# Infini-attention plus SiLU layer on one core: tile 2 of x issued from ScalarE, VectorE's constants made behind the norms

## The chip, the core and the metric

The kernel runs on one core of one Trainium2 chip. A core has five engines with instruction queues of their own, each of which runs in program order: TensorE (PE; its weight loads are shown as PEld), VectorE (DVE), ScalarE (ACT), GpSimd (POOL) and SyncE (SP), which here only issues transfers. ScalarE can issue transfers as well. Engines wait for each other and for transfers through semaphores. The metric is the device time of one execution in microseconds (us); the time of a kernel is the median over several runs.

## The reference, cut to what matters

A sequence of 2048 tokens of width 512 is normalised; an attention with 32 heads of width 16, in four segments of 512 tokens with a memory that is carried from segment to segment, and a dense layer with SiLU both read the normalised x, and both are added to x.

```python
x = A_x
xn = _layernorm(x, axis=-1)
return x + _A_ref(xn, A_wq, A_wk, A_wv, A_wo, A_beta) + _B_ref(xn, B_w1, B_w2)
...
for s in range(N):
    qs, ks, vs = (q[:, :, s].copy(), k[:, :, s].copy(), v[:, :, s].copy())
    p = _softmax(jnp.einsum('bhqd,bhkd->bhqk', qs, ks) * scale + mask, axis=-1)
    a_dot = jnp.einsum('bhqk,bhkd->bhqd', p, vs)
    pq = phi(qs)
    num = jnp.einsum('bhld,bhde->bhle', pq, M)
    den = jnp.einsum('bhld,bhd->bhl', pq, z)[..., None] + 1e-06
    outs.append(g * num / den + (1.0 - g) * a_dot)
    pk = phi(ks)
    M = M + jnp.einsum('bhld,bhle->bhde', pk, vs)
    z = z + jnp.einsum('bhld->bhd', pk)
...
out = jnp.einsum('bsf,fd->bsd', _silu(jnp.einsum('bsd,df->bsf', x, w1)), w2)
```

x, the weights and the result are bf16; wq, wk, wv and wo are 512 x 512, w1 is 512 x 1792 and w2 1792 x 512.

## The kernel before

x is cut into 16 tiles of 128 tokens, four to a segment. Each tile is normalised on VectorE, turned so that its 512 channels lie on partitions (`xnT`), and multiplied with wq, wk, wv and w1 in pieces of 128 channels. The scores of a segment are made in batches, go through an exponential on ScalarE (line 730), are masked on GpSimd (line 744) and weigh v (line 791). Everything is accumulated in on-chip banks and copied out by VectorE or ScalarE.

The order of work is a list written out by hand, `ORDER`. Each word is a piece of work: a short function that issues one instruction or a few, on one or more engines. Each engine then executes its own instructions in the order of the list. The words that matter here are these:

- `xc`, `xd`: the statistics of a tile and their aggregate, on VectorE (lines 286 and 289); `xs` does both at once; `xq`, `xi`: square root on ScalarE (line 303) and reciprocal on VectorE (line 306); `Nv`: the normalised tile, on VectorE (line 315). `xg4.4` makes the roots of tiles 4 to 7 together on GpSimd (lines 297 and 300), and `xs4` to `xs7` are their statistics.
- `X`, `Xa`, `Xv`: the transposes of a tile on TensorE (line 845), and their copies into `xnT` on ScalarE or VectorE (line 851).
- `busy`: matmuls on zeros that fill TensorE's time (line 864). `busy44` stands ahead of the first transposes, `X0.1`.
- `v`, `k`, `q`, `h`: products of line 336; `vv`, `va`, `kv`, `ka`, `qv`, `qa`: their copies on VectorE or ScalarE (lines 376, 399 and 406). `kf0.0` splits the first k (lines 392 and 393) and needs `pm_odd` and `pm_even`; `kp` does the same on GpSimd for later ones.
- `S`: a batch of scores; `E`, `O`: weighted sums.
- `kind`: five small VectorE instructions on 128 x 1 numbers (lines 239 to 246), first used for the sums of the denominators; `odd`: the two reductions that make `pm_odd` and `pm_even` (lines 223 and 224); `omask`: one conversion of `pm_odd` (line 235), first used when the odd sums are merged (line 835).
- `ones0`, `ones1`, `zeros`: memsets on GpSimd.

Ahead of the list stand the loads. Tiles 0 to 3 are loaded one by one by `load_x`, 128 KB each, in turn from SyncE's queue and ScalarE's. On SyncE's queue follow wv in two halves, wk, wq, tiles 4 to 7 (`x_hi`), w1 in two halves, tiles 8 to 11 and 12 to 15, and beta, each issued as soon as a semaphore of an earlier transfer is free. ScalarE loads its table and runs one activation ahead of its first use (line 190) after its own issues; VectorE clears `zraw` (line 188) and `lows` (line 262) ahead of the list.

Of the kernel before, what the change touches and what calls it, by code (L numbers as in the profile page):

```python
# [13 lines left out]


ORDER = """
kind odd omask ones0 ones1 zeros xc0 xd0 xc1 xq0 xi0 Nv0 busy44 xd1 xq1 xc2 xi1 X0.1 Nv1 xd2 Xa0.1 busy6 v0.0.0 v0.0.1 xq2 X1.1 Xa1.1 xs3 xi2 Nv2 v0.0.2 xq3 v0.0.3 xi3 v0.1.0 v0.1.1 Nv3 X2.1 va0.0 k0.0.0 k0.0.1 tb Xv2.1 X3.1 v0.1.2 v0.1.3 Xv3.1 vv0.1 k0.1.0 k0.0.2 k0.0.3 ka0.0 fp0.0 kf0.0 q0.0.0 q0.0.1 q0.0.2 q0.0.3 xs4 k0.1.1 qa0.0 k0.1.2 k0.1.3 kv0.1 fa0.0 xs7
S0 k0.3.0 fa0.1 k0.2.0 k0.2.1 k0.2.2 k0.2.3 kv0.2 k0.3.1 k0.3.2 q0.1.0 xs5 xs6 xg4.4 fv0.0 k0.3.3 kv0.3
S2 q0.1.1 v0.2.0 kp0.1 q0.1.2 q0.1.3 qv0.1 v0.2.1 v0.2.2 v0.2.3 vv0.2 fa0.2 Nv6 Nv4 XD6 XD4 h0.0.0 h0.0.1
S1 Nv5 XD5 h0.0.2 h0.0.3 ha0.0 hv0.0 h0.1.0 h0.1.1 fp0.2 h0.1.2 h0.1.3 q0.2.0  # L20
S3 q0.2.1 q0.2.2 q0.3.0 q0.3.1 q0.3.2 q0.2.3 Nv7 qv0.2 ha0.1 h0.2.0 h0.2.1 kp0.2 q0.3.3
# [72 lines left out]
def kernel(  # L94
# [13 lines left out]
    nc = tc.nc  # L108
# [10 lines left out]
    TPS = L // P  # L119
# [24 lines left out]
    def xs(t0, t1):  # L144
        if t0 >= NT - TPS:
            return x_end[:, t0 - NT + TPS : t1 - NT + TPS, :]
        return x_lo[:, t0:t1, :] if t1 <= TPS else x_hi[:, t0 - TPS : t1 - TPS, :]
# [9 lines left out]
    def load_x(eng, t0, n):  # L157
        eng.dma_start(
            out=xs(t0, t0 + n),
            in_=x_flat[t0 * P : (t0 + n) * P, :].rearrange("(n p) d -> p n d", p=P),  # L160
        )

    load_x(nc.sync, 0, 1)
    load_x(nc.scalar, 1, 1)
    load_x(nc.sync, 2, 1)
    load_x(nc.scalar, 3, 1)

    def load_w(eng, w_sb, W, k0, k1):
        eng.dma_start(out=w_sb[:, k0:k1, :], in_=W.rearrange("(ko ki) n -> ki ko n", ki=P)[:, k0:k1, :])
# [45 lines left out]
    kind = cpool.tile([P, 1], F32, name="kind")  # L215
# [16 lines left out]
    omask = cpool.tile([P, 1], I32, name="omask")  # L232
# [710 lines left out]
```

## Time and profile before

| | |
|---|---|
| median of 3 runs | 221.12 us (220.74 to 221.27) |
| the profiled execution | 220.8 us, of which the span from its first to its last instruction is 219.1 us |
| TensorE busy | 211.6 us, 4019 matmuls |
| ScalarE busy | 184.2 us |
| VectorE busy | 181.0 us |
| GpSimd busy | 126.8 us |
| granted TensorE clock | 1.00 |
| transfers | 19.60 MB, mean 89 GB/s |

The page gives busy time by engine, then the chain of waits: from the last instruction back, at each step to what released it. A row of the timeline has the start and the length in us, the engine, the line, the operation, the tile written and the tiles read, their sizes and the count; in brackets stands the idle time of the engine ahead of it and what ended that. Rows of an engine overlap a little where its instructions are pipelined. Windows give the busy time of each engine in a stretch of the span.

### The profile page before, as it was taken

How to read it: one execution, taken by the hardware profiler on the slowest of the kernel's cores; microseconds unless marked ns; L12 is line 12 of the kernel's file. 1: busy time of each engine (PE TensorE's matmuls, PEld its weight loads, DVE VectorE, ACT ScalarE, POOL GpSimd, SP SyncE). 2: the span in 40 equal slices, each digit the busy share in tenths (PEclk: the TensorE clock that was granted, in tenths of full speed). 3: DMA queues.
4: the chain of work that ended last, by engine and by line, in shares of the span. 5: the costliest groups of instructions: out<-in, count | busy, mean ns of one | idle time of the engine just before them, and what ended most of it. 6: DMA issues, size and time to landing. Idle time of an engine off the chain costs nothing.

```text
span 219.1 us, 9343 instructions
## 1 busy us (share of the span) xinstructions
PE 211.6 (97%) x4019; PEld 116.3 (53%) x4042; DVE 181.0 (83%) x370; ACT 184.2 (84%) x173; POOL 126.8 (58%) x203
## 2 busy tenths in 40 slices
PE   7999999999999999999999999999999999999994
PEld 7666655556544544445544445455454544465663
DVE  7899999999897878757988979777899798669364
ACT  3899989999999999999999999999999988860000
POOL 6039986679687845695845486667768473410000
PEclk9999999999999999999999999999999999999999
DMA  6994549242003035321122142160032221322313
GB/s 197 357 372 128 79 129 344 42 79 46 4 4 75 25 86 71 83 62 29 51 74 61 43 121 28 47 79 7 4 99 75 75 76 45 97 60 76 97 52 97
DMA packets 33273, 19.60 MB, mean 89 GB/s; under 512 B 14672, under 2 KB 33232, under 8 KB 33232
## 3 DMA queue, kind: packets, MB, share of 16 engines
q1 hardware_dynamic: 30608, 16.39, 29.1%
q10 hardware_dynamic: 2624, 2.62, 3.7%
q8 instruction: 31, 0.51, 1.0%
q14 instruction: 10, 0.08, 0.1%
HBM read 9.96 MB, written 2.10 MB: 55 GB/s over the span
## 4 chain that ended last, share of the span: by engine, by line
PE 82%; DVE 9%; POOL 4%; issue 2%; ACT 1%
PE ps L336 20%; PE psO L338 16%; PE ps L338 15%; PE psS L724 9%; PE psO L336 9%; PE psV L791 8%; PE psS L338 4%; DVE stats L286 2%; POOL Pb L744 2%; DVE Vz L406 1%; POOL k L385 1%; DVE hT L497 1%; DVE pk L433 1%; POOL lows L744 1%; PE ptr L845 1%
## 5 line engine op out<-in xcount | busy, mean ns | idle before, releaser
L730 ACT ACTIVATE Pb<-psS 128x2048 bf16<-128x2048 f32 x72 | 135.2, 1877 | 6.3 <-PE psS L724 4.1
L744 POOL TENSOR_SCALAR_AFFINE_SELECT Pb<-Pb 128x512 bf16<-128x512 bf16 (+2 forms) x88 | 61.6, 710 | 19.2 <-ACT Pb L730 16.5
L497 DVE SCALAR_TENSOR_TENSOR hT<-th,ps 128x512 bf16<-128x512 bf16 x56 | 38.0, 681 | 10.6 <-ACT th L492 10.2
L744 POOL TENSOR_SCALAR_AFFINE_SELECT lows<-Pb 64x512 bf16<-64x512 bf16 (+1 forms) x40 | 23.2, 581 | 37.5 <-ACT Pb L730 31.1
L338 PE MATMUL psO<-w_sb,hT 128*32 128x512 bf16 (+2 forms) x708 | 43.3, 321 | 0.0
L336 PE MATMUL ps<-xnT,w_sb 128*128 128x512 bf16 (+1 forms) x165 | 34.2, 329 | 0.4 <-DVE Vz L406 0.2
L492 ACT ACTIVATE th<-ps 128x512 bf16<-128x512 f32 x56 | 33.2, 594 | 1.7 <-PE ps L338 1.6
L338 PEld LDWEIGHTS <-hT 128*32 128x32 bf16 x876 | 21.6, 97 | 14.0 <-issue 2.6
L338 PE MATMUL ps<-xnT,w_sb 128*32 128x512 bf16 (+1 forms) x448 | 26.4, 348 | 0.0
L724 PE MATMUL psS<-qT,k 32*128 32x64 bf16 (+3 forms) x512 | 23.0, 233 | 0.5 <-ACT Pb L730 0.3
L336 PEld LDWEIGHTS <-w_sb 128*128 128x128 bf16 x168 | 15.8, 98 | 11.4 <-issue 1.0
L791 PE MATMUL psV<-Pb,Vz 128*32 128x448 bf16 (+7 forms) x512 | 21.6, 286 | 0.2 <-POOL Pb L744 0.2
L724 PEld LDWEIGHTS <-k 32*128 32x128 bf16 x512 | 9.4, 92 | 22.8 <-issue 22.2
L336 PE MATMUL psO<-w_sb,hT 128*128 128x512 bf16 (+2 forms) x82 | 20.9, 326 | 0.6 <-issue 0.5
L791 PEld LDWEIGHTS <-Vz 128*32 128x32 bf16 x768 | 16.2, 97 | 9.2 <-issue 0.8
L621 DVE SCALAR_TENSOR_TENSOR o_out<-psO,x_res 128x512 bf16<-128x512 f32 x14 | 9.6, 689 | 6.6 <-PE psO L338 4.9
L338 PEld LDWEIGHTS <-w_sb 128*32 128x32 bf16 x448 | 11.2, 96 | 7.3 <-issue 1.6
L724 PE MATMUL psS<-qT,kT 16*128 16x448 bf16 (+3 forms) x256 | 14.7, 269 | 0.0
L821 DVE CAST oraw<-psV 128x512 bf16<-128x512 f32 x15 | 10.2, 682 | 3.1 <-PE psV L791 3.0
L406 DVE CAST Vz<-ps 128x512 bf16<-128x512 f32 x15 | 10.2, 682 | 2.8 <-PE ps L338 1.6
L336 PEld LDWEIGHTS <-hT 128*128 128x128 bf16 x89 | 7.8, 98 | 8.7 <-issue 2.2
L336 PE MATMUL ps<-xnT,wq_sb 128*128 128x256 bf16 (+1 forms) x59 | 12.1, 322 | 0.2 <-issue 0.2
(113 smaller groups left out, 333.5 us busy)
## 6 DMA issues: line engine op xcount, KB each, us to landing
spr<-rz SPq DMA_DIRECT2D x56, 64.0 KB
x_res<-in_A_x_dram SPq DMA_DIRECT2D x16, 128.0 KB
out_dram<-o_out SPq DMA_DIRECT2D x15, 128.0 KB
w_sb<-in_B_w_dram SPq DMA_DIRECT2D x2, 896.0 KB
w_sb<-in_B_w_dram ACTq DMA_DIRECT2D x1, 1792.0 KB
x_hi<-in_A_x_dram SPq DMA_DIRECT2D x2, 512.0 KB
wv_sb<-in_A_wv_dram SPq DMA_DIRECT2D x2, 256.0 KB
wk_sb<-in_A_wk_dram SPq DMA_DIRECT2D x1, 512.0 KB
```

The source lines that it names most:

```text
L286: nc.vector.bn_stats(out=stats[t][:], in_=xs(t, t + 1)[:, 0, :])
L336: return [nc.tensor.matmul(out, lhsT=lhsT, rhs=rhs, start=start, stop=stop, skip_group_check=True)]
L338: nc.tensor.matmul(out[c : c + 32], lhsT=lhsT[:, c : c + 32], rhs=rhs, start=start, stop=stop, tile_position=(0, c), skip_group_check=True,)
L406: copy(out=Vzs[s % 2][:, j, :, 0:3:2, :], in_=sts[s].pop(("v", j))[:, :].rearrange("p (h r d) -> p h r d", r=2, d=DH),)
L492: nc.scalar.activation(out=th[:], in_=sts[s]["h", ft][:, :], func=AF.Tanh, scale=0.5)
L497: nc.vector.scalar_tensor_tensor(out=st["hT"][:, ft, :], in0=st.pop(("th", ft))[:], scalar=1.0, in1=st.pop(("h", ft))[:, :], op0=ALU.add, ...
L621: out = nc.vector.scalar_tensor_tensor(out=o_out[:], in0=st.pop(("psO", j)), scalar=0.5, in1=st["x", j][:], op0=ALU.mult, op1=ALU.add)
L724: nc.tensor.matmul(psS[:, g, c : c + q2 - q1], lhsT=keys[rows], rhs=st["qT"][rows, dt, q1:q2], start=True, stop=True, tile_position=(32 * ...
L730: exp = nc.scalar.activation(out=blocks(Pb, b).rearrange("p y g c -> p g y c"), in_=psS[:, :, :].rearrange("p g (y c) -> p g y c", c=BLOCK ...
L744: over[id(Pb)].append(nc.gpsimd.affine_select(out=out, in_=in_, compare_op=ALU.is_ge, fill=0.0, base=base, pattern=[[0, out.shape[1]], [1, ...
L791: nc.tensor.matmul(psV[32 * g : 32 * g + 32, q0 : q0 + nq].rearrange("p (y c) -> p y c", y=weights.shape[2]), lhsT=Vzs[s % 2][:, kt, 4 * d ...
L821: copy(out=oraw[:], in_=sts[s].pop(("psV", 0))[:, :])
```

## The change

Two edits. First, tile 2 of x is no longer issued by SyncE behind tile 0 but by ScalarE behind tile 1; ScalarE issues tiles 1, 2 and 3, and wv is second on SyncE's queue. Second, the words `kind`, `odd` and `omask` leave the head of the list. `odd` goes behind `Xv3.1`, the copy of tile 3's transposes; `omask` and `kind`, in this order, go behind `S0`, the first batch of scores. On VectorE that puts `odd` between the copy of tile 3 and the copy `vv0.1`, and `omask` and `kind` between the statistics of tile 7 (`xs7`) and the copy `kv0.2`. All other words keep their order, and TensorE's, GpSimd's and ScalarE's own instructions keep theirs but for the extra issue. Long lines of the list are cut.

```diff
 ORDER = """
-kind odd omask ones0 ones1 zeros xc0 xd0 xc1 xq0 xi0 Nv0 busy44 xd1
+ones0 ones1 zeros xc0 xd0 xc1 xq0 xi0 Nv0 busy44 xd1
...
-v0.1.2 v0.1.3 Xv3.1 vv0.1 k0.1.0 k0.0.2 k0.0.3 ka0.0 fp0.0 kf0.0
+v0.1.2 v0.1.3 Xv3.1 odd vv0.1 k0.1.0 k0.0.2 k0.0.3 ka0.0 fp0.0 kf0.0
...
 q0.0.0 q0.0.1 q0.0.2 q0.0.3 xs4 k0.1.1 qa0.0 k0.1.2 k0.1.3 kv0.1 fa0.0 xs7
-S0 k0.3.0 fa0.1 k0.2.0 k0.2.1 k0.2.2 k0.2.3 kv0.2 k0.3.1 k0.3.2 q0.1.0 xs5 xs6 xg4.4 fv0.0 k0.3.3 kv0.3
+S0 omask kind k0.3.0 fa0.1 k0.2.0 k0.2.1 k0.2.2 k0.2.3 kv0.2 k0.3.1 k0.3.2 q0.1.0 xs5 xs6 xg4.4 fv0.0 k0.3.3 kv0.3
...
     load_x(nc.sync, 0, 1)
-    load_x(nc.scalar, 1, 1)
-    load_x(nc.sync, 2, 1)
-    load_x(nc.scalar, 3, 1)
+    for t in range(1, TPS):
+        load_x(nc.scalar, t, 1)
```

More of the change, by code (lines that the diff above doesn't have):

```diff
@@ L16 @@
 ORDER = """
-kind odd omask ones0 ones1 zeros xc0 xd0 xc1 xq0 xi0 Nv0 busy44 xd1 xq1 xc2 xi1 X0.1 Nv1 xd2 Xa0.1 busy6 v0.0.0 v0.0.1 xq2 X1.1 Xa1.1 xs3 xi2 Nv2 v0.0.2 xq3 v0.0.3 xi3 v0.1.0 v0.1.1 Nv3 X2.1 va0.0 k0.0.0 k0.0.1 tb Xv2.1 X3.1 v0.1.2 v0.1.3 Xv3.1 vv0.1 k0.1.0 k0.0.2 k0.0.3 ka0.0 fp0.0 kf0.0 q0.0.0 q0.0.1 q0.0.2 q0.0.3 xs4 k0.1.1 qa0.0 k0.1.2 k0.1.3 kv0.1 fa0.0 xs7
-S0 k0.3.0 fa0.1 k0.2.0 k0.2.1 k0.2.2 k0.2.3 kv0.2 k0.3.1 k0.3.2 q0.1.0 xs5 xs6 xg4.4 fv0.0 k0.3.3 kv0.3
+ones0 ones1 zeros xc0 xd0 xc1 xq0 xi0 Nv0 busy44 xd1 xq1 xc2 xi1 X0.1 Nv1 xd2 Xa0.1 busy6 v0.0.0 v0.0.1 xq2 X1.1 Xa1.1 xs3 xi2 Nv2 v0.0.2 xq3 v0.0.3 xi3 v0.1.0 v0.1.1 Nv3 X2.1 va0.0 k0.0.0 k0.0.1 tb Xv2.1 X3.1 v0.1.2 v0.1.3 Xv3.1 odd vv0.1 k0.1.0 k0.0.2 k0.0.3 ka0.0 fp0.0 kf0.0 q0.0.0 q0.0.1 q0.0.2 q0.0.3 xs4 k0.1.1 qa0.0 k0.1.2 k0.1.3 kv0.1 fa0.0 xs7
+S0 omask kind k0.3.0 fa0.1 k0.2.0 k0.2.1 k0.2.2 k0.2.3 kv0.2 k0.3.1 k0.3.2 q0.1.0 xs5 xs6 xg4.4 fv0.0 k0.3.3 kv0.3
 S2 q0.1.1 v0.2.0 kp0.1 q0.1.2 q0.1.3 qv0.1 v0.2.1 v0.2.2 v0.2.3 vv0.2 fa0.2 Nv6 Nv4 XD6 XD4 h0.0.0 h0.0.1
```

## The prediction, made before the changed kernel ran

> **What bounds the kernel now.** I read the page's first part, then its chain of waits, then the same chain from 10 to 46 us, then the timeline of the first 17 us, where every moved instruction lies.
>
> ```profile
> span 219.1 us, 9343 instructions
> PE 211.6 (97%) x4019; PEld 116.3 (53%) x4042; DVE 181.0 (83%) x370; ACT 184.2 (84%) x173; POOL 126.8 (58%) x203
> PE 82%; DVE 9%; POOL 4%; issue 2%; ACT 1%
> ```
>
> TensorE is busy for 97% of the span and carries 82% of the chain that ended last. The windows of busy time (engines in the order PE, PEld, DVE, ACT, POOL, then clock, DMA share, GB/s) show where the other 18% can come from:
>
> ```profile
> 38.00:120.00 82.00, 80.86 (x1535) 41.72 (x1548) 68.87 (x138) 80.47 (x70) 57.68 (x89) 1.00 0.24 54
> 120.00:200.00 80.00, 79.42 (x1594) 40.59 (x1596) 67.16 (x131) 71.46 (x65) 45.46 (x71) 1.00 0.25 61
> ```
>
> From 38 to 200 us TensorE idles 1.1 us of 82 and 0.6 of 80. Its order is fixed, so a time won or lost before 38 us has no idle stretch to vanish in: I carry it to the end one to one. The question is what sets the start of that packed part. The chain in order of time (start, length, what):
>
> ```profile
> 13.68 0.02 issue
> 13.71 0.69 DVE kT L376
> ...
> 16.10 0.58 POOL rstd_all L297
> ...
> 25.59 1.10 POOL Pb L744
> ...
> 27.07 0.69 DVE oraw L821
> ...
> 37.10 0.61 DVE Vz L406
> 37.71 0.14 issue
> 37.85 1.91 PE ps L336 x15
> ```
>
> So before 13.68 the chain is TensorE and ScalarE, from 13.71 to 16.0 it is VectorE, from 16.10 to 26.7 GpSimd, from 27 to 37.7 VectorE, and then TensorE. The stretch 13.71 to 16.0 is the one the change touches: the copy kv0.2, the statistics xs5 and xs6, and behind them GpSimd's root xg4.4.
>
> **The change part by part.** The head first (timeline, start and length in us):
>
> ```profile
> 1.10 4.17 PE L864 MATMUL psS<-zraw 128*128 128x128 bf16 x44 [1.10 <-DVE zraw L188]
> 1.40 1.23 DVE L262 MEMSET lows<- 64x1408 uint32 x1 [0.35 <-issue]
> 2.66 0.22 DVE L239 TENSOR_REDUCE kind<-ident 128x1 f32<-128x64 bf16 x1
> 2.91 0.15 DVE L243 TENSOR_SCALAR evec<-kind 128x1 f32<-128x1 f32 x1
> 2.98 0.14 DVE L244 TENSOR_SCALAR evec<-kind 128x1 f32<-128x1 f32 x1
> 3.16 0.16 DVE L245 TENSOR_TENSOR evec<-evec,evec 128x1 f32<-128x1 f32 x1
> 3.24 0.15 DVE L246 TENSOR_SCALAR sign<-kind 128x1 f32<-128x1 f32 x1
> 3.30 0.15 DVE L223 TENSOR_REDUCE pm_odd<-b 128x1 f32<-128x4 f32 x1
> 3.48 0.15 DVE L235 CAST omask<-pm_odd 128x1 int32<-128x1 f32 x1
> 3.56 0.68 DVE L286 BATCH_NORM_STATS2 stats<-x_lo 128x6 f32<-128x512 bf16 x1
> 5.55 0.66 DVE L286 BATCH_NORM_STATS2 stats<-x_lo 128x6 f32<-128x512 bf16 x1
> 5.60 0.40 PE L845 MATMUL ptr<-ident,xn_t 128*128 128x128 bf16 x4 [0.32 <-DVE xn_t L315]
> 6.73 0.66 DVE L286 BATCH_NORM_STATS2 stats<-x_lo 128x6 f32<-128x512 bf16 x1
> ```
>
> Eight small instructions stand between the memset, which ends at 2.63, and tile 0's statistics at 3.56: VectorE could start 0.9 us sooner. Two things cap that. TensorE first runs its 44 filler matmuls, which end at 5.27; the transposes of tile 0 start at 5.60, so TensorE can gain 0.33 us at most. And tile 0 must have landed. The windows from the start give bytes:
>
> ```profile
> 0.00:2.70 2.70, 1.59 (x16) 1.60 (x17) 1.44 (x3) 0.99 (x1) 1.90 (x12) 1.00 0.30 103
> 0.00:3.70 3.70, 2.60 (x25) 2.60 (x26) 2.37 (x11) 1.49 (x2) 2.90 (x13) 1.00 0.51 153
> 0.00:4.70 4.70, 3.60 (x37) 3.60 (x38) 3.33 (x13) 1.63 (x3) 3.48 (x15) 1.00 0.60 181
> 0.00:9.90 9.90, 8.26 (x81) 6.50 (x83) 8.09 (x29) 5.57 (x12) 3.48 (x15) 1.00 0.83 267
> ```
>
> By 2.70 us 2.7 x 103 = 278 kB are in, tiles 0 and 1 (262 kB); so tile 0 lands between 2.7 and 3.56. The full 0.33 us needs its statistics by 3.56 - 0.33 = 3.23, inside that interval and nearer its middle than its end: I take 0.33, with nothing as the other end.
>
> Tile 2 leaves SyncE's queue for a third place on ScalarE's. These rows say what an issue costs and who stands behind it:
>
> ```profile
> 0.78 0.90 ACTq L158 DMA_DIRECT2D x_lo<-in_A_x_dram  x2
> 0.79 0.87 SPq L158 DMA_DIRECT2D x_lo<-in_A_x_dram  x2
> 1.71 1.28 ACT L190 ACT_TABLE_LOAD   x1 [1.71 <-PEq L927]
> 4.55 0.29 ACT L303 ACTIVATE rstd_all<-mv_all,eps 128x1 f32<-128x1 f32 x1 [1.35 <-DVE mv_all L289]
> ```
>
> An issue is about 0.45 us. ScalarE's table load and its first activation move from 1.71 to 2.16 and end near 3.65; the first root, at 4.55 - 0.33 = 4.22, does not feel it. Without that cover of 0.57 us the 0.45 would go into tile 0's path. On SyncE everything behind tile 0 (wv, wk, wq, x_hi, w1 and the rest) is issued 0.44 us earlier. If both queues get equal shares, tile 2 is in after tiles 0 and 1, itself and as much of wv: 524 kB, 3.6 us by the second row; tile 3 after 786 kB, 4.4 us by the third (851 kB at 4.70). Their statistics, now at 5.55 and 6.73, would start at 5.22 and 6.40. Both are covered, tile 2 by 1.6 us less its landing delay. That delay is bounded by tile 0's: 0 to 0.86.
>
> Of the constants the two sums of pm_odd and pm_even (3.30 to 3.48, so 0.18 us) go behind the copy Xv3.1. They cost nothing, because VectorE waits 0.61 us just after; the other six go to the bad place (VectorE, 11 to 16 us):
>
> ```profile
> 11.04 0.35 DVE L392 TENSOR_SCALAR k<-kT,pm_odd 128x512 bf16<-128x512 bf16 x1 [0.61 <-ACT kT L376]
> 11.30 0.69 DVE L286 BATCH_NORM_STATS2 stats<-x_hi 128x6 f32<-128x512 bf16 x1
> 13.42 0.18 DVE L289 BATCH_NORM_AGGREGATE mv_all<-stats 128x2 f32<-128x6 f32 x1
> 15.03 0.18 DVE L289 BATCH_NORM_AGGREGATE mv_all<-stats 128x2 f32<-128x6 f32 x1
> 15.13 0.66 DVE L286 BATCH_NORM_STATS2 stats<-x_hi 128x6 f32<-128x512 bf16 x1
> 16.10 0.57 POOL L297 TENSOR_SCALAR rstd_all<-mv_all 128x4 f32<-128x4 f32 x1 [0.45 <-DVE mv_all L289]
> ```
>
> Omask and the five of kind now stand between the aggregate at 13.42 and kv0.2 at 13.71. They take, start to start, 3.30 - 2.66 = 0.64 for kind and 3.56 - 3.48 = 0.08 for omask: 0.72 us. Unpipelined, their lengths add up to 0.97; I take 0.72, since the same six issue back to back again. The idle time there: an aggregate's successor can start 0.10 us after it (15.03 to 15.13), so kv0.2 could have started at 13.52 and waited 0.19 for TensorE. The rest of the cover is the head's gain as far as VectorE still has it. It loses some at 11.30, since xs4 needs x_hi. Tiles, wv, wk, wq and x_hi are 5 x 524 kB = 2.62 MB, in by 9.9 us (267 x 9.9 = 2.64), so x_hi lands between 9.9 and 11.30; s, what xs4 can move forward, lies between 0.33 and 0. I take 0.2, near the middle, for want of a row that shows the landing.
>
> The sum at kv0.2: 0.72 - 0.19 - 0.2 = +0.33 us; its ends are 0.72 - 0.19 - 0.33 = +0.20 and 0.97 - 0.19 - 0 = +0.78. A gain is excluded as long as those six instructions must run there: 0.72 exceeds 0.19 + 0.33. Behind kv0.2 VectorE has no gap up to xs6, and GpSimd has already idled 0.45 us for xg4.4; so its chain to 26.7, VectorE's to 37.7 and TensorE's start at 37.85 each come 0.33 later. That makes the span 219.4, the profiled execution 221.1 (now 220.8 around a span of 219.1), and, against the median of the three runs, which is 0.3 above the profiled one, 221.4.
>
> One rule speaks against expecting more of the freed SyncE queue. The Trainium skill (DMA: Bandwidth & Descriptors, Issuing engines are not separate DMA queues) says that transfers started by different engines interleave on the same DMA engines, and that a second issuing engine saves issue time alone. The trace agrees: from 3.70 to 9.90 us the DMA share was (9.9 x 0.83 - 3.7 x 0.51) / 6.2 = 1.02, full. By the rule x_hi lands no earlier than today; if the 0.44 us of issue did bring it forward, s would be 0.33 and the sum +0.20.
>
> **The rivals.** Slower: tile 3 arrives late behind two others on ScalarE's queue. If SyncE's queue, always full, took three quarters of the engines at 300 GB/s, tiles 2 and 3 would pass at 75 GB/s from 2.7 us: 2 x 131 kB take 3.5 us, to 6.2, and with 0.86 for landing tile 3 is there at 7.06, 0.33 behind today's 6.73. The head is then 0.33 later instead of earlier, and kv0.2 is 0.72 - 0.19 + 0.33 = +0.86: 222.0. It decides once tile 3's statistics start after 6.73. For it: nothing in the trace shows how two full queues share; against: two tiles to a queue, all four were in by 3.70 (566 kB against 524).
>
> Faster: the VectorE stretch isn't what releases the packed part, GpSimd and VectorE catch up, and TensorE keeps its head gain: 0.33 less, 220.8. For it: VectorE is only 9% of the chain, and up to 13.68 TensorE sets it. Against: the 0.45 us that GpSimd waited for exactly these statistics, and no pause in GpSimd's chain of 10 us.
>
> The change doesn't do what it says: tile 0 lands only at about 3.56, the head gains nothing, and the constants cost 0.72 - 0.19 = +0.53: 221.65. For it: nothing shows the landing; against: 278 kB by 2.70.
>
> **How the numbers follow.** Forecast 0.58, no head gain 0.10, late tile 0.15, head gain kept 0.12; 0.05 for what I don't see, on either side. A measurement of this kernel can tell about 0.3%, 0.66 us, from no change. Of the forecast a tenth lies above that (its upper end is +0.78), and the late tile does: with half of the unseen, slower 0.24. A gain of 0.66 is twice the head's cap: half of the unseen and a quarter of the kept head, where one measurement also falls low, make faster 0.06. The same is left with 0.70. The forecast with its ends is 221.3 to 221.9 by the median; 220.6 to 222.1 takes in the kept head gain and the late tile.
>
> **What would show it.** Right: tile 0's statistics near 3.2 and the first transposes near 5.27; six small instructions between xs7's aggregate and kv0.2; kv0.2 near 14.04, GpSimd's root near 16.43, TensorE's long group near 38.2, and the same distance at the end. Wrong: statistics of tile 3 after 6.73 (late tile); kv0.2 at 13.8 or before, or the root late with the group at 37.85 on time (head gain kept); first transposes still at 5.60 (no head gain). A shift that grows after 38 us would break the one-to-one step.

## The result, and the profile after

The changed kernel takes 222.10 us (median of 12 runs, 221.61 to 223.21) against 221.18 us of the kernel before in the same session: a ratio of 1.0047 with an interval of 1.0034 to 1.0060. By the ratio it is 1.04 us slower (0.0047 x 221.2), by the two medians 0.92; +0.33 was forecast.

The first part of the changed kernel's page (all its line numbers are one lower than before's, since the calls of `load_x` lost a line; kernels with the old loads have before's numbers, and those that load halves have numbers seven higher):

```profile
span 220.8 us, 9345 instructions
PE 212.2 (96%) x4019; PEld 117.0 (53%) x4042; DVE 180.8 (82%) x370; ACT 184.2 (83%) x173; POOL 126.9 (57%) x203
```

The profiled execution took 222.54 us. The span is 1.7 us longer; TensorE is busy 0.6 us longer and the other three as long as before within 0.2. What grew is mostly waiting. Its chain of waits from 5 to 46 us, in order of time (start, length, what):

```profile
1.72 6.09 DMA x_lo<-in_A_x_dram
7.84 0.71 DVE stats L285
...
9.30 0.40 PE ptr L844 x4
...
11.51 0.60 ACT kT L375
...
15.36 0.60 DVE kT L375
...
17.66 0.57 POOL rstd_all L296
...
28.83 0.69 DVE oraw L820
...
39.60 1.91 PE ps L335 x15
```

The same stations as before, each later: the first copy of kT on ScalarE 11.51 for 10.42, the root 17.66 for 16.10, the first weighted sum `oraw` 28.83 for 27.07, the long group 39.60 for 37.85. Between the copy on ScalarE and `oraw` lies kv0.2, which starts at 15.28 in the timeline; the chain shows only its part from 15.36. The changed kernel's timeline (start, length, engine, line, operation, tiles, count, in brackets what ended the idle time before):

```profile
3.29 0.69 DVE L285 BATCH_NORM_STATS2 stats<-x_lo 128x6 f32<-128x512 bf16 x1 [0.66 <-DMA x_lo<-in_A_x_dram]
5.65 0.39 PE L844 MATMUL ptr<-ident,xn_t 128*128 128x128 bf16 x4
7.84 0.69 DVE L285 BATCH_NORM_STATS2 stats<-x_lo 128x6 f32<-128x512 bf16 x1 [1.28 <-DMA x_lo<-in_A_x_dram]
9.30 0.40 PE L844 MATMUL ptr<-ident,xn_t 128*128 128x128 bf16 x4 [0.90 <-DVE xn_t L314]
14.51 0.18 DVE L288 BATCH_NORM_AGGREGATE mv_all<-stats 128x2 f32<-128x6 f32 x1
14.61 0.12 DVE L234 CAST omask<-pm_odd 128x1 int32<-128x1 f32 x1
15.21 0.15 DVE L245 TENSOR_SCALAR sign<-kind 128x1 f32<-128x1 f32 x1
15.28 0.68 DVE L375 CAST kT<-ps 128x512 bf16<-128x512 f32 x1
17.66 0.56 POOL L296 TENSOR_SCALAR rstd_all<-mv_all 128x4 f32<-128x4 f32 x1 [0.92 <-DVE mv_all L288]
```

Three things are to be seen. The head did not get shorter: the statistics of tile 0 start 0.27 sooner, the first transposes 0.05 later. Tile 3's statistics wait 1.28 us for their transfer, to 7.84. And from 14.61 to 15.28, for 0.67 us, the six constants stand ahead of kv0.2, with GpSimd's root waiting 0.92 us instead of 0.45.

Cut at the three stations, the profiled executions differ by 1.09 us up to kT on ScalarE (11.51 - 10.42), 0.48 from there to kv0.2 (3.77 - 3.29), 0.19 from kv0.2 to `oraw` (13.55 - 13.36) and nothing behind it (220.8 - 28.83 = 192.0, and 219.1 - 27.07 = 192.0). These are single executions; the runs tell which of the parts hold in the median.

### The profile page after: what moved, and what is told of

The parts are those of the page before. It is cut to its first block, busy times and chain, and to the rows that moved or that the text cites. A ratio compares the mean times of both kernels' runs of the same rounds, so it can differ in the third digit from the quotient of the medians.

```text
span 220.8 us, 9345 instructions
## 1 busy us (share of the span) xinstructions
PE 212.2 (96%) x4019; PEld 117.0 (53%) x4042; DVE 180.8 (82%) x370; ACT 184.2 (83%) x173; POOL 126.9 (57%) x203
## 4 chain that ended last, share of the span: by engine, by line
PE 80%; DVE 9%; POOL 4%; DMA 3%; issue 2%; ACTq 0%; ACT 0%
PE ps L335 19%; PE psO L337 16%; PE ps L337 14%; PE psO L335 9%; PE psS L723 9%; PE psV L790 8%; PE psS L337 4%; DMA x_lo<-in_A_x_dram 3%; DVE stats L285 2%; POOL Pb L743 2%; DVE Vz L405 1%; DVE hT L496 1%; POOL k L384 1%; DVE pk L432 1%; DVE mv_all L288 1%
## 5 line engine op out<-in xcount | busy, mean ns | idle before, releaser
L416 POOL TENSOR_SCALAR pos<-kT 128x512 bf16<-128x512 bf16 x12 | 7.7, 645 | 8.3 <-ACT kT L375 7.9
```

The source lines that it names most:

```text
L416: nc.gpsimd.tensor_scalar(out=pos[:], in0=phi_src(s, of, dt), scalar1=3.0e38, scalar2=0.0, op0=ALU.min, op1=ALU.max)
```

## The experiments

All are timed against the kernel before in the same session (its medians there: 221.15 to 221.22 us). The last columns are read from each kernel's one profiled execution: the start of the first kT copy on ScalarE, the time from there to kv0.2, from kv0.2 to the first `oraw`, and from there to the end of the span.

| run | median us | ratio [95%] | kT | to kv0.2 | to oraw | to end |
|---|---|---|---|---|---|---|
| before | 221.18 | 1 | 10.42 | 3.29 | 13.36 | 192.0 |
| after | 222.10 | 1.0047 [1.0034, 1.0060] | 11.51 | 3.77 | 13.55 | 192.0 |
| e5_after_again | 221.85 | 1.0037 [1.0022, 1.0051] | 10.53 | 3.86 | 13.56 | 192.0 |
| e1_loads | 221.20 | 1.0002 [0.9990, 1.0014] | 10.77 | 3.28 | 13.37 | 192.0 |
| e2_consts | 221.87 | 1.0032 [1.0021, 1.0043] | 11.18 | 3.82 | 13.56 | 191.9 |
| e3_late | 221.16 | 0.9999 [0.9986, 1.0012] | 10.98 | 3.28 | 13.36 | 192.0 |
| e14_loads_late | 221.16 | 1.0001 [0.9984, 1.0017] | 12.05 | 3.29 | 13.38 | 192.0 |
| e4_x3_sync | 221.81 | 1.0034 [1.0023, 1.0044] | 11.24 | 3.83 | 13.55 | 191.9 |
| e6_nv2_first | 222.23 | 1.0048 [1.0031, 1.0064] | 11.14 | 3.77 | 13.56 | 192.0 |
| e7_behind_root | 221.78 | 1.0020 [1.0011, 1.0030] | 11.19 | 3.29 | 13.63 | 192.0 |
| e8_k_later | 221.54 | 1.0013 [1.0003, 1.0023] | 11.22 | 3.29 | 13.39 | 192.0 |
| e9_wk_behind_wq | 222.66 | 1.0063 [1.0045, 1.0081] | 11.52 | 3.28 | 13.37 | 191.9 |
| e10_halves | 220.93 | 0.9990 [0.9978, 1.0001] | 10.42 | 3.29 | 13.37 | 192.1 |
| e11_halves_late | 221.12 | 0.9997 [0.9986, 1.0007] | 10.53 | 3.29 | 13.36 | 192.2 |
| e12_halves_late_fill | 221.03 | 0.9998 [0.9983, 1.0013] | 10.50 | 3.29 | 13.36 | 192.1 |
| e13_pk_behind | 222.06 | 1.0046 [1.0028, 1.0063] | 10.12 | 4.01 | 13.61 | 192.1 |
| e15_pk_behind_alone | 221.48 | 1.0016 [1.0007, 1.0024] | 10.45 | 3.42 | 13.59 | 192.1 |

The last four columns add up to the span of that one execution. So the scatter of the column kT, from 10.12 to 12.05, is real time, but it is one draw for each kernel and does not follow the medians. Among kernels that the same edit touches, the two columns behind it repeat to about 0.1 us (4.01 of e13_pk_behind apart, which has a reason of its own below).

**The change taken apart.** e1_loads has the edit of the loads with the old list. e2_consts has the edit of the list with the old loads. e3_late has the old loads and the list with the constants off the chain:

```diff
-S0 omask kind k0.3.0
+S0 k0.3.0
-ha0.8 hv0.8
+ha0.8 omask hv0.8
-kv2.1 hv0.12
+kv2.1 kind hv0.12
```

> The load edit alone: tiles 1, 2 and 3 on ScalarE's queue, the constants at the head as before. Late tile: tile 3, third on ScalarE's queue, lands past 6.7 us in many executions; its statistics wait for the transfer, the transposes of tile 2 stand behind them, and the median is 0.5 to 1.0 us above before, 221.7 to 222.2, with a wider spread between runs than before. Constants: what costs is their new place, so the loads alone change nothing, -0.1 to +0.2 us.

> The list edit alone: the constants behind the norms, the loads as before. Late tile: nothing arrives late, the six constants ahead of kv0.2 cost 0.72 - 0.19 less what the head gains, so +0.2 to +0.5 us. Constants: the whole of the change's cost comes from here, +0.8 to +1.1 us.

> The loads as before and the list edit, but omask ahead of hv0.8 and kind ahead of hv0.12, where VectorE waits 0.22 and 0.53 us in the profile of before. Late tile: with no constants between xs7 and kv0.2 and all tiles early, the head's gain of up to 0.33 us is kept: -0.3 to 0. Constants: taking them off the chain from 13.7 us on gives the same -0.3 to 0, so this run tests the head alone: if the fillers of TensorE end near 5.6 us as in the profile of the changed kernel, and not at 5.27, the gain is nothing.

The edit of the loads alone makes no difference that can be measured (1.0002). The edit of the list alone costs 0.32%, 0.71 us, which lies between its two expectations (up to 0.5, and 0.8 or more). With the constants off the chain, the eight instructions have left the head as in the change, and the time is that of before (0.9999, 0.9986 to 1.0012): no gain of the head shows. So the place of the six constants costs 0.7 us, and nothing that can be seen pays for it. Why e3_late has no gain is in its profile, first the timeline, then the chain:

```profile
3.60 0.69 DVE L286 BATCH_NORM_STATS2 stats<-x_lo 128x6 f32<-128x512 bf16 x1 [0.97 <-DMA x_lo<-in_A_x_dram]
```

```profile
3.78 8.17 DMA x_hi<-in_A_x_dram
11.95 0.02 issue
11.98 0.71 DVE stats L286
```

VectorE stands idle for 0.97 us, and tile 0 is there only at 3.60, later than before's 3.56; and tile 4's statistics start when x_hi has landed, at 11.95. So two loads stand in the way in this execution, the first of them at the very start.

**Tile 3 and the queue.** e4_x3_sync is the changed kernel with two tiles to a queue again; e6_nv2_first makes tile 2's normalisation independent of tile 3's arrival; e5_after_again is the changed kernel itself, in that session.

```diff
-    for t in range(1, TPS):
-        load_x(nc.scalar, t, 1)
+    load_x(nc.scalar, 1, 1)
+    load_x(nc.scalar, 2, 1)
+    load_x(nc.sync, 3, 1)
```

```diff
-xs3 xi2 Nv2
+xi2 Nv2 xs3
```

> The changed kernel with tile 3 taken back to SyncE's queue, behind tile 0; tiles 1 and 2 on ScalarE's. Two tiles to a queue again. Late tile: tile 3's statistics start near 6.4 and do not wait for the transfer; what is left is the constants' price, +0.2 to +0.5 us above before. Constants: nothing changes against the changed kernel, +0.9 to +1.1 us.

> The changed kernel once more, beside the next three. Stream: the head waits for wk in nearly every execution whatever comes ahead of it, so tile 3's place costs little and the time is that of the list edit alone, +0.7 us above before. Late tile: tile 3 behind two others costs 0.3 us on top, +1.0 us again.

> The changed kernel with Nv2 ahead of xs3, so that tile 2's normalisation and transposes no longer stand behind statistics that wait for tile 3. Stream: no difference to the changed kernel, +0.7 us above before. Late tile: 0.2 to 0.3 us less than the changed kernel in the same session.

With tile 3 on SyncE the ratio is 1.0034, 0.75 us, again between its two expectations. Without, it is 1.0047 in the first session, 1.0037 in e5's and 1.0048 with the reordering of e6: the intervals overlap, and the reordering gained nothing. What was left open went into e14_loads_late, the new loads with e3's list.

> The loads of after with the list in which the constants lie off the chain (odd behind Xv3.1, omask ahead of hv0.8, kind ahead of hv0.12). Theory (the load edit costs nothing): 1.000, as with the old loads. Rival (tile 3's third place on ScalarE's queue costs 0.2 to 0.3 us in the median): 1.001 to 1.0014, with its statistics at 7.6 or later in the profile.

Its median is 1.0001, as e3's. But its profiled execution, at 222.49 the longest of its 12, shows what the late tile does when it happens. Its timeline:

```profile
8.38 0.69 DVE L285 BATCH_NORM_STATS2 stats<-x_lo 128x6 f32<-128x512 bf16 x1 [1.61 <-DMA x_lo<-in_A_x_dram]
9.85 0.40 PE L844 MATMUL ptr<-ident,xn_t 128*128 128x128 bf16 x4 [1.53 <-DVE xn_t L314]
```

Tile 3 is there only at 8.38, 1.65 later than before's 6.73, and the transposes of tile 2, whose reciprocal and normalisation stand behind those statistics, wait 1.53 us. That execution is 1.3 us above the kernel's median; ten of its twelve runs lie between 220.41 and 221.25. So the late tile is real, and it strikes some executions, not the median one (the interval of this kernel, 0.9984 to 1.0017, leaves room for up to 0.4 us either way).

**What sets the head.** The first products with wk follow the transposes of tile 2. The rows of those products in three profiled executions, of e2_consts, e1_loads and, further below, e9_wk_behind_wq:

```profile
9.20 0.61 PE L336 MATMUL ps<-xnT,wk_sb 128*128 128x256 bf16 x4 [0.73 <-DMA wk_sb<-in_A_wk_dram]
```

```profile
8.78 0.61 PE L335 MATMUL ps<-xnT,wk_sb 128*128 128x256 bf16 x4 [0.20 <-DMA wk_sb<-in_A_wk_dram]
```

The same row of before's timeline has no wait:

```profile
8.42 0.60 PE L336 MATMUL ps<-xnT,wk_sb 128*128 128x256 bf16 x4
```

e8_k_later puts those products behind v's last ones, so that TensorE has something else to do; e9_wk_behind_wq exchanges the loads of wk and wq, so that wk is later; e10_halves loads the column halves of wk and wq that are used first ahead of x_hi and the others behind it, so that wk's first half is earlier.

```diff
-X2.1 va0.0 k0.0.0 k0.0.1 tb Xv2.1 X3.1 v0.1.2 v0.1.3 Xv3.1
+X2.1 va0.0 tb Xv2.1 X3.1 v0.1.2 v0.1.3 k0.0.0 k0.0.1 Xv3.1
```

```diff
-    load_w(nc.sync, wk_sb, A_wk, 0, 4)
     load_w(nc.sync, wq_sb, A_wq, 0, 4)
+    load_w(nc.sync, wk_sb, A_wk, 0, 4)
```

```diff
-    load_w(nc.sync, wk_sb, A_wk, 0, 4)
-    load_w(nc.sync, wq_sb, A_wq, 0, 4)
+    load_half(wk_sb, A_wk, 0)
+    load_half(wq_sb, A_wq, 0)
     load_x(nc.sync, 4, 4)
+    load_half(wk_sb, A_wk, 1)
+    load_half(wq_sb, A_wq, 1)
```

> The kernel before with one move: k0.0.0 and k0.0.1, the first products that need wk, behind v0.1.3, so that tile 3's transposes and 0.6 us of v products run while wk is under way. Stream: TensorE's wait for wk (0.2 to 0.7 us in three of the profiles so far) is filled, -0.2 to -0.4 us. Rival, the head is bound by its own instructions and not by wk: 0 to +0.4 us, since tile 3's transposes then wait for its normalisation.

> The kernel before with wk and wq loaded in the other order, so that wk lands about 524 kB, 1.4 us, later. Stream: the head waits for wk already, so the time grows by nearly all of it, +1.2 to +1.5 us. Rival, wk has slack against the head's own instructions: under +0.6 us.

> The kernel before with wk and wq loaded in halves by columns; the first halves, which k0.0, k0.1, q0.0 and q0.1 read, stay in front, the second halves go behind x_hi. The first half of wk lands about 0.7 us earlier, that of wq and x_hi 1.4 us. Stream: the head comes down to what its instructions take, -0.2 to -0.4 us. Rival: -0.1 to +0.1 us.

The timelines of e9_wk_behind_wq, e10_halves and e8_k_later:

```profile
9.53 0.61 PE L336 MATMUL ps<-xnT,wk_sb 128*128 128x256 bf16 x4 [0.85 <-DMA wk_sb<-in_A_wk_dram]
```

```profile
8.42 0.60 PE L343 MATMUL ps<-xnT,wk_sb 128*128 128x256 bf16 x4
```

```profile
9.26 0.40 PE L845 MATMUL ptr<-ident,xn_t 128*128 128x128 bf16 x4 [0.28 <-DVE xn_t L315]
```

A later wk costs 0.63%, 1.4 us, about all of the delay that was expected for it, so in the median wk lands at about the time when TensorE comes to need it. An earlier wk gains 0.1%, 0.2 us, the small end of what was expected, with an interval that touches no change. Its one profile has no wait and starts these products at 8.42, as before's does; its 11 runs lie closer together (220.86 to 221.34) than before's 29 beside them (220.76 to 221.96). e8 went the way of its rival: without the products ahead of them the transposes of tile 3 wait for its normalisation, and the kernel is 0.13% slower. So wk and the head's own instructions are nearly balanced in the kernel before, and a gain on one of them alone meets the other.

If wk were the only thing that hides the head's gain, the gain should appear with wk early and the constants off the chain: e11_halves_late has e10's loads and e3's list, e12_halves_late_fill 36 fillers for 44 as well.

> The same loads, and the constants out of the head (omask ahead of hv0.8, kind ahead of hv0.12, odd behind Xv3.1). Stream: with wk early the head's own gain shows where the fillers end early, 0 to 0.3 us below the run with the halves alone, so -0.3 to -0.6 us below before. Fillers: if TensorE's 44 fillers, which ended between 5.0 and 6.0 us in the profiles so far, hold up the transposes more often than tile 0's normalisation, no difference to the halves alone.

> The same again with 36 fillers for 44, which end 0.45 to 0.85 us earlier. Fillers: the transposes start when tile 0 is normalised, near 5.25 us, in every execution: 0.2 to 0.4 us below the run before this one. Stream alone: no difference to it.

Both missed: 0.9997 and 0.9998. The timeline of e11_halves_late shows the next two waits:

```profile
3.32 0.69 DVE L293 BATCH_NORM_STATS2 stats<-x_lo 128x6 f32<-128x512 bf16 x1 [0.70 <-DMA x_lo<-in_A_x_dram]
6.59 0.38 PE L343 MATMUL ps<-wv_sb,xnT 128*128 128x512 bf16 x1 [0.48 <-DMA wv_sb<-in_A_wv_dram]
```

Tile 0's statistics start 0.24 sooner than before and the first transposes 0.22 (5.38), and then TensorE waits 0.48 us for wv. In e12_halves_late_fill the fillers are out of the way as well, and tile 0 itself comes late:

```profile
3.52 0.69 DVE L293 BATCH_NORM_STATS2 stats<-x_lo 128x6 f32<-128x512 bf16 x1 [0.89 <-DMA x_lo<-in_A_x_dram]
```

Behind tile 0, wv and wk stands x_hi, as e3's chain above and e13's below show.

**The constants elsewhere.** e7_behind_root puts them behind GpSimd's root, ahead of fv0.0, where VectorE has 0.47 us of idle time later on, ahead of `oraw`.

```diff
-S0 omask kind k0.3.0
+S0 k0.3.0
-xs6 xg4.4 fv0.0
+xs6 xg4.4 omask kind fv0.0
```

> The loads as before and the list edit, but omask and kind behind xg4.4, so that the same six instructions follow tile 7's neighbours' statistics and no longer hold up GpSimd's root. Chain as predicted: VectorE waits about 0.5 us for the first weighted sums at 27 us, which takes them in, so 0 to +0.2 us above before. Rival, VectorE packed from 13 to 37 us so that they cost anywhere in it: +0.5 to +0.7 us.

The way to kv0.2 is as before, 3.29, but 0.27 us are lost between kv0.2 and `oraw`, and 0.20% in the time, 0.44 us, between its two expectations: that idle time does not hide them all. VectorE comes to its second `pk` (24.38 there, 22.96 in before) 0.65 us later after kv0.2 than before, this `pk` takes 0.91 for 0.82, and `oraw` follows without a wait: 0.65 + 0.09 less the idle 0.47 is the 0.27. The constants also hold up ScalarE, whose exponential `ex` waits for the first `pk`:

```profile
18.10 0.63 ACT L423 ACTIVATE ex<-kT 128x512 bf16<-128x512 bf16 x1 [0.53 <-DVE pk L433]
```

**GpSimd's 0.2 us.** In every kernel with the constants ahead of kv0.2 the stretch from kv0.2 to `oraw` is 0.2 longer, though none of its instructions changed. Two GpSimd rows and one VectorE row of before's timeline, and the same of the changed kernel's with the VectorE row behind `pk`:

```profile
22.45 0.79 POOL L744 TENSOR_SCALAR_AFFINE_SELECT Pb<-Pb 128x256 bf16<-128x256 bf16 x2
22.96 0.82 DVE L433 SCALAR_TENSOR_TENSOR pk<-ex,pos 128x512 bf16<-128x512 bf16 x1
23.32 1.02 POOL L385 TENSOR_SCALAR k<-kT,pm_odd 128x512 bf16<-128x512 bf16 x1
```

```profile
24.01 1.32 POOL L743 TENSOR_SCALAR_AFFINE_SELECT Pb<-Pb 128x256 bf16<-128x256 bf16 x2
24.37 0.69 DVE L432 SCALAR_TENSOR_TENSOR pk<-ex,pos 128x512 bf16<-128x512 bf16 x1
24.98 0.08 DVE L432 DVE_READ_ACCUMULATOR pk<-ex,pos 128x1 f32 x1
25.41 0.69 POOL L384 TENSOR_SCALAR k<-kT,pm_odd 128x512 bf16<-128x512 bf16 x1
```

GpSimd's instruction that is due while VectorE makes `pk` is the long one: the k with 1.02 for 0.69 before, the second small select after (the pair 1.32 for 0.79). The losses are 0.33 and 0.53, and their difference is the 0.2. e13_pk_behind (e2's kernel) and e15_pk_behind_alone (before's) move `pk` behind tile 10's statistics:

```diff
-hv0.1 XD7 fv0.2 fa0.3 h0.2.2 v0.3.0 v0.3.1 v0.3.2 t0.0 t0.2 xs10
+hv0.1 XD7 xs10 fv0.2 fa0.3 h0.2.2 v0.3.0 v0.3.1 v0.3.2 t0.0 t0.2
```

> The list edit with the loads of before, and tile 10's statistics (xs10) ahead of the feature sum fv0.2 instead of behind it, so VectorE's pk starts some 0.8 us later (near 24.9 instead of 24.1). Theory (GpSimd's instruction that meets pk on VectorE is held until pk ends): the two small selects go back from 1.31 to 0.79, and the k of pm_odd or of pm_even that now meets pk becomes long (1.0 for 0.69, or 0.9 for 0.48); from kv0.2 to the first oraw copy 13.4 to 13.7. Rival (the selects are long for a reason of their own, such as their data or their distance from the root): they stay at 1.3. Time by either: 1.002 to 1.0035.

> The kernel of before with xs10 ahead of fv0.2 and nothing else; VectorE's pk starts near 23.8 instead of 22.96. Theory (the instruction that meets pk is held): selects 0.79 and k of pm_odd 0.7 instead of 1.02, k of pm_even 0.9 instead of 0.47; the first oraw copy 0.1 later to 0.1 sooner. Rival: pm_odd stays at 1.02. Time 0.9995 to 1.001 by either.

The timelines of e13_pk_behind and e15_pk_behind_alone:

```profile
22.88 0.79 POOL L744 TENSOR_SCALAR_AFFINE_SELECT Pb<-Pb 128x256 bf16<-128x256 bf16 x2
23.74 0.69 POOL L385 TENSOR_SCALAR k<-kT,pm_odd 128x512 bf16<-128x512 bf16 x1
24.04 0.93 DVE L433 SCALAR_TENSOR_TENSOR pk<-ex,pos 128x512 bf16<-128x512 bf16 x1
24.41 0.91 POOL L385 TENSOR_SCALAR k<-kT,pm_even 128x256 bf16<-128x256 bf16 x1
```

```profile
23.46 0.69 POOL L385 TENSOR_SCALAR k<-kT,pm_odd 128x512 bf16<-128x512 bf16 x1
24.13 0.91 POOL L385 TENSOR_SCALAR k<-kT,pm_even 128x256 bf16<-128x256 bf16 x1
```

The long instruction went with `pk` in both: the selects are back at 0.79, the k of pm_odd takes 0.69, and the k of pm_even, the one that now meets `pk`, takes 0.91 for 0.47. So it is shown that `pk` holds up the GpSimd instruction that meets it. The Trainium skill (SBUF — State Buffer, Who interferes with whom) says that a VectorE instruction with two inputs in SBUF, an on-chip memory, contends with a GpSimd instruction that reads it, and that the lock on the ports that they share is exclusive. The rows agree: in the changed kernel the second select ends at 24.01 + 1.32 = 25.33, and at the 0.39 that it takes undisturbed (half of 0.79) it ran from 24.94, when `pk` was nearly over (the row behind it starts at 24.98).

The times are another matter, and both missed. e15 lost 0.16%, 0.35 us, where at most 0.1% was expected, and e13's ratio is 1.0046, where 1.002 to 1.0035 was expected (its interval reaches down to 1.0028). What the later `pk` costs stands on ScalarE, whose `ex` waits for it; e15's row and the same of before:

```profile
24.80 0.63 ACT L423 ACTIVATE ex<-kT 128x512 bf16<-128x512 bf16 x1 [0.77 <-DVE pk L433]
```

```profile
23.89 0.62 ACT L423 ACTIVATE ex<-kT 128x512 bf16<-128x512 bf16 x1
```

The chain of e15 runs from `pk` over `ex` and `th` to the next exponentials of the scores, and `oraw` comes 0.23 us later after kv0.2; so before's order is the better one. Another 0.13 of e15's execution belongs to a wait of 0.23 for x_hi, after which tile 4's statistics start at 11.65, with nothing in the head changed. In e13 `ex` waits 0.82; whether more than chance sets its ratio 0.14% above e2's stays open, and their intervals overlap. One more thing is seen in e13's profile, the execution with the earliest head of all (first transposes 5.30, kT 10.12). Its chain from 8 to 16 us:

```profile
3.76 7.45 DMA x_hi<-in_A_x_dram
11.21 0.02 issue
11.23 0.71 DVE stats L286
```

Here the head's 0.30 us were gained, and tile 4's statistics wait for x_hi until 11.21: they start 0.07 sooner than before's 11.30.

## Why the prediction missed, step by step

- *Constants ahead of kv0.2, 0.72 - 0.19 = 0.53:* right. From kT to kv0.2 the changed kernel takes 0.48 longer (0.67 for the six instructions, less the 0.19), its repetition 0.57, e2 0.53, e4 0.54.
- *The head's gain, 0.33 at the transposes and s = 0.2 at tile 4, "near the middle, for want of a row that shows the landing":* this is the step that failed. No gain shows in the median: e3, e11, e12 and e14 take the eight constants off the head without putting the six on the chain, and stand at 0.9997 to 1.0001. Each of these intervals is 0.2 to 0.4 us wide on either side, so one alone does not exclude 0.2; the traces say why there is none. The sum took tile 0 as landed by 3.23, since 278 kB were in by 2.70; but by then all four tiles and wv had been issued, so the count does not tell whose bytes these are. In the eleven profiled executions with the constants out of the head tile 0's statistics always wait for their transfer and start at 3.21 to 3.60, at 3.42 in the middle one: 0.14 sooner than before, not 0.33. The first transposes start at 5.30 to 5.77, in the middle at 5.56, 0.04 sooner.
- *The loads behind tile 0,* the same step further on: of these only x_hi was counted, as a cap on s. Followed back from 14 us, the chain of all eleven goes to a transfer, wk in five (e2, e4 to e7), wv in two (e11, e12), tile 3 in two (the changed kernel and e14) and x_hi in two (e3, e13), where before's goes to VectorE's own work at the head. x_hi, which was to land between 9.9 and 11.30, was there at 11.21 in e13, where it capped the gain at 0.07, and at 11.95 in e3. The profiled execution of before shows no wait for wk at all, at 8.42, and that was read as a fixed fact. TensorE's fillers are the same case: their row ends at 5.27 there and at 1.10 + 4.71 = 5.81 in the changed kernel, where the first transposes, whose row overlaps it a little, start at 5.65, though tile 0's normalisation was done 0.36 before that (4.88 + 0.41 = 5.29).
- *GpSimd's chain, VectorE's and TensorE's start "each come 0.33 later", GpSimd's unchanged in length:* wrong by +0.2, a term that the sum lacked. A shift of VectorE against GpSimd moved `pk` from the k onto the selects. With it and without s the sum is 0.53 + 0.20 = 0.73, against 0.71 for the list alone.
- *One to one to the end:* right; from `oraw` to the end every kernel takes 191.9 to 192.2. The changed kernel's windows (columns as in the prediction's) are those of before within 0.2 us of TensorE's time:

```profile
38.00:120.00 82.00, 80.70 (x1539) 41.82 (x1543) 68.97 (x139) 80.50 (x71) 57.55 (x89) 1.00 0.24 60
120.00:200.00 80.00, 79.42 (x1578) 40.38 (x1587) 67.51 (x131) 73.04 (x67) 47.06 (x73) 1.00 0.25 61
```

- *The freed SyncE queue:* no gain was counted on it, and e1's 1.0002 agrees. The rule of the Trainium skill that was weighed there (DMA: Bandwidth & Descriptors, Issuing engines are not separate DMA queues), that a second issuing engine saves issue time alone, fits this.
- *The rival of the late tile:* its sign was there in the changed kernel's own profile (7.84, past the 6.73 that decides), and in e14's (8.38), with a price in that execution above the 0.33 that was worked out. It is not what made up most of the loss: with the constants off the chain the same loads give 1.0001.
- *The rival without head gain, +0.53, given a tenth of the chance:* its price is what came, with GpSimd's 0.2 on top. Its reason, tile 0 at about 3.56, held in part of the executions only (3.50 to 3.60 in e3, e12 and e14); in the others later loads did the same. That the median lies at the upper end of the wider range, 222.1, is luck: this end was put there for the late tile.

What stays open is the rest of the changed kernel's 1.04 us. Accounted for are 0.73; its repetition gave 0.82 (0.0037 x 221.2) and the two intervals reach from 0.5 to 1.3 us, so the rest may be nothing or some 0.3. Executions with a late tile 3 raise it at times (two of the 12 runs lie above 222.8), but no run separates this from chance.

No kernel here is clearly faster than before; the nearest is e10_halves with 0.9990, an interval up to 1.0001 and the narrowest spread.

## What to carry to other kernels

A head that waits for loads is a race between transfers, and one profiled execution shows one outcome of it. A count of bytes does not tell which of the transfers under way has landed. Where no wait is seen, ask how far behind the next transfer is before counting a gain on an engine, and count none that has to pass two or three landings. Small instructions cost their length where the next engine already waits for what stands behind them, so they go where nobody waits, not where the engine looks idle a little later. When VectorE is shifted against GpSimd, look which GpSimd instructions will then run beside a VectorE instruction with two inputs in on-chip memory.

## What the runs showed of the hardware that was not expected

The first product with wk started between 8.42 without a wait and 9.20 after one of 0.73 us with the same loads (before and e2). The 44 fillers ended at 5.00 us in one execution (e11) and at 5.99 in another (e3), with a granted clock of 1.00 from 1.10 to 6.00 us in both; why was not tried. Tile 0, the first transfer on its queue, was ready at 3.24 in one execution and at 3.60 in another with the same loads (e13 and e3). Another 128 KB tile, third on its queue, was ready at 6.40 at the latest in one execution of the changed kernel (e5) and at 7.84 in another, and at 8.38 with the same loads in e14. VectorE's `pk`, a sum of two tiles, cost the GpSimd instruction beside it 0.33 to 0.53 us, and was itself 0.82 to 0.93 us long for 0.69 where it came second.
